# A state-space block ahead of an MLP: where one chunk's decay banks, its score and mix products and a set of transposes stand in the queues

## The chip, the core and the metric

The kernel runs on one core of a Trainium2 chip. A core has five engines with a queue each: PE (matrix products; its weight loads are listed apart as PEld), DVE (VectorE), ACT (ScalarE), POOL (GpSimd) and SP, which here only starts transfers. Each engine works through its own queue in the order in which the program issued it, and waits at an instruction until what it needs is there. PE writes into PSUM, eight banks of 128 x 512 float32 values; DVE and ACT read them there.

The metric is the device time of one execution in microseconds (us). Before the change it is 372.75 us, the median of 6 runs (371.79 to 374.67).

## What is computed

Inputs are x (4 batches, 8 heads, 768 tokens, 32 values), a decay `a` for each batch, head and token, and B and C with 16 state values for each. The reference works in chunks of tokens:

```python
log_a = np.log(np.clip(a, 1e-06, 1.0))
cum = np.cumsum(la, axis=-1)                      # la: log_a of the chunk
L = np.exp(cum[:, :, :, None] - cum[:, :, None, :]) * causal
CB = np.einsum('bhin,bhjn->bhij', Cc, Bc)
y_intra = np.einsum('bhij,bhjd->bhid', CB * L, xc)
y_inter = np.einsum('bhin,bhnd->bhid', Cc, state) * decay_to_i[:, :, :, None]
y[:, :, sl] = y_intra + y_inter                   # and the state is carried on
```

The result, 3072 tokens of 256 values, goes through an MLP: h = y @ w_in (256 to 2048), g = h * clip(h + 3, 0, 6) / 6, out = g @ w_out (2048 to 256). The weights come as float64 and are turned into float32 on the chip.

## The kernel before

It takes 6 chunks of 128 tokens for all 4 batches at once, and works the MLP of chunk k beside the attention of chunk k+1. The order on every engine is the order of the program (`tc.manual_schedule()`, L68); tiles of one tag share a fixed number of buffers, and a new tile waits until the one whose room it takes is no longer read.

**PSUM.** Tag "f" has four banks, "o" two, "y0" and "y1" one each. [...]

**Decays of chunks 0 and 1.** L is kept as [token j, head, token i], a pair of batches to a tile. For chunk 0 and for batches 0 and 1 of chunk 1 it is made by PE: a bank `d` holds half of a batch's heads (b is the batch, u the half). `diff_mask` (L272) chooses the bank and writes the causal mask; `diff_add` (L286) adds the differences of the running sums in five small matmuls; `diff_exp` (L297) is ACT's exponential into L. Chunk 0's banks are f, f, f, f, o, o, y0, y1; chunk 1's are all "o". `diff_fill(b, u)` (L711) is mask and add for chunk 1, `diff` (L678) all three at once.

**Attention of chunk 0.** `turn(0, p)` (L335) transposes B and C of two batches into one "f" bank (eight transposes for both p) and copies them out: `bT` by ACT, `cT` by DVE for p = 0 and by ACT for p = 1. `scores(0, (b,))` (L369) makes the products of C and B for one batch in four "f" banks `cb` (32-row matmuls), and DVE multiplies them into L (L384). `mix(0, (b,))` (L387) multiplies L with x into the two "y" banks, 32 columns at a time. `keep(0, p)` (L423) has ACT copy two batches to `yT` and DVE take the new state. `ends` (L317) is POOL's product for that state.

**Weights.** `weights(i, n)` (L673) takes n steps of `decode(i)` (L154): (1) ACT copies the top words, (2) three DVE operations, (3) an ACT pass, (4) an ACT pass and a DVE product (L178), after which `load_w(i + 3)` is issued on SP, (5) two DVE operations, of which the last writes a quarter of w_in (i below 4) or w_out. Three raw buffers are used in turn.

**MLP of chunk 0.** `mlp_in(0, f)` (L445) makes one of 16 blocks of h with four matmuls of w_in on PE; ACT and DVE make gT of it (L524, L529). The list `weave` puts decode steps between the blocks. `first_out` (L533) multiplies gT with w_out into `o`. The tile gT of chunk 0 takes the room of `pre` (tag "gT", one buffer), in which the running sums `cum` of all chunks lie.

**by_token** (L260) has PE transpose the running sums of chunks 1 to 5 out of `pre` (five small transposes into one "o" bank, `c_ps`), and DVE write them negated to `cum_n`, which the exponentials of later chunks read from batch 2 of chunk 1 on (L312). In the kernel before it stands in the MLP of chunk 0 behind block f = 1.

The sequence around the change (L698 to L740) is written out by hand:

Of the kernel before, what the change touches and what calls it, by code (L numbers as in the profile page):

```python
# [20 lines left out]
def kernel(  # L21
# [238 lines left out]
    def by_token():  # L260
        c_ps = ps_o.tile([P, NC, G], FP32, name="c_ps", tag="o")
        for c in range(1, NC):
            nc.tensor.transpose(out=c_ps[:, c], in_=cum_c[:, c], identity=ident[:G, :G])
        nc.vector.tensor_scalar(
            out=cum_n[:, 1:], in0=c_ps[:, 1:], scalar1=-1.0, scalar2=None, op0=ALU.mult)
# [6 lines left out]
    def diff_mask(c, b, u):  # L272

        k = 2 * b + u
        if c == 0 and k < 4:
            d = ps.tile([P, HU, P], FP32, name="d", tag="f")
        elif c == 0 and k >= 6:
            d = ps_y.tile([P, HU, P], FP32, name="d", tag=f"y{u}")
        else:
            d = ps_o.tile([P, HU, P], FP32, name="d", tag="o")  # L280
        nc.tensor.matmul(
            out=d, lhsT=ident_h, rhs=hide.unsqueeze(1).to_broadcast([P, HU, P]),
            start=True, stop=True)
        ds[c, b, u] = d
# [12 lines left out]
    def diff_exp(c, b, u):  # L297
        nc.scalar.activation(
            decays_of(c, b)[:, HU * u:HU * u + HU], ds.pop((c, b, u)), AF.Exp)
# [14 lines left out]
    def from_start(c):  # L314
        nc.scalar.activation(etos[c], etos[c], AF.Exp)
# [19 lines left out]
    def turn(c, p):  # L335


        bc, xt = loaded[c]
        pool, tag = (ps, "f") if c < 2 else (ps_o, "o")
        t_ps = pool.tile([P, 4, P], FP32, name="t_ps", tag=tag)  # L340
        for k in range(4):
            j, b = k // 2, 2 * p + k % 2
            nc.tensor.transpose(  # L343
                out=t_ps[:, k],
                in_=bc[:, j, b * NH:(b + 1) * NH].rearrange("s h n -> s (h n)"), identity=ident)
        bT = att.tile([P, 2, P], FP32, name="bT")
        nc.scalar.copy(out=bT, in_=t_ps[:, 2:4])
        if c == 1 and p == 0:
            from_start(c)
            carry(c)  # L350
            for b in range(NB):
                ends(c, b)
        cT = att.tile([P, 2, 2, P], FP32, name="cT")
        if c == 1 or (c, p) == (0, 1):
            for t in range(2):
                nc.scalar.activation(
                    cT[:, :, t], t_ps[:, 0:2], AF.Copy, scale=parity[:, t:t + 1])
        else:
            nc.vector.tensor_tensor(
                out=cT, in0=t_ps[:, 0:2].unsqueeze(2).to_broadcast([P, 2, 2, P]),  # L360
                in1=parity.unsqueeze(1).unsqueeze(3).to_broadcast([P, 2, 2, P]), op=ALU.mult)
        csT = None
        if c:
            csT = att.tile([P, 2, P], FP32, name="csT")
            nc.vector.tensor_tensor(
                out=csT, in0=t_ps[:, 0:2], in1=etos[c][:, 2 * p:2 * p + 2], op=ALU.mult)
        bTs[c, p] = bT, cT, csT
# [305 lines left out]
    def weights(i, n):  # L673
        for _ in range(n):
            next(parts[i], None)


    def diff(c, b, u):  # L678
        diff_mask(c, b, u)
        diff_add(c, b, u)  # L680
        diff_exp(c, b, u)
# [20 lines left out]
    ends(0, 0)  # L702
    diff_exp(0, 1, 0)
    weights(0, 2)
    for b, u in ((2, 0), (2, 1), (1, 1), (3, 0)):
        diff_exp(0, b, u)
    for b in range(NB - 1):
        ends(0, b)
# [2 lines left out]
    def diff_fill(b, u):  # L711
        diff_mask(1, b, u)
        diff_add(1, b, u)

    diff_fill(0, 0)
    diff_fill(0, 1)
    turn(0, 0)
    turn(0, 1)
    diff_exp(0, 3, 1)
    ends(0, 3)  # L720
    diff_exp(1, 0, 0)
    diff_exp(1, 0, 1)
    weights(1, 1)
    scores(0, (0,))
    scores(0, (1,))
# [2 lines left out]
    mix(0, (1,))  # L728
    keep(0, 0)
    scores(0, (3,))  # L730
    diff(1, 1, 0)
    mix(0, (2,))
    mix(0, (3,))
    weights(1, 1)
    diff_fill(1, 1)
    keep(0, 1)
    diff_exp(1, 1, 1)
    weights(1, 3)
    load_eto(1)
    load(1)  # L740
# [7 lines left out]
    for k in range(NC):  # L748
        gTs[k] = ffn.tile([P, NF, TB], FP32, name="gT")
        c, ahead = k + 1, k + 2  # L750
        if k == 0:
            for f in range(NF):
                mlp_in(k, f)
                for i in weave.get(f, []):
                    weights(i, 1)
                if f == 1:
                    by_token()
                if f in (6, 8):
                    b = f // 2 - 1
                    load_decay(c, b)  # L760
                    conceal(c, b)
            load(ahead)
            weights(NP + 1, 1)
            weights(NP + 3, 1)
            weights(NP + 2, 3)
            sums, sums_in = weight_sums(), in_weight_sums()
            for i in range(NP):
                for b in range(NB):
                    first_out(b, i)
                    if (i, b) == (0, 0):  # L770
                        weights(NP + 3, 1)
                        weights(NP + 2, 1)
                        weights(NP + 3, 3)
                        rows(ahead)
                        decay(c, 2)
                        decay(c, 3)
                    elif (i, b) == (1, 0):
                        next(sums_in)
                    elif (i, b) == (2, 0):
                        turn(c, 0)  # L780
                        turn(c, 1)
                        for b_ in range(NB):
                            conceal(ahead, b_)
                    elif (i, b) == (2, 1):
                        scores(c, (0, 1))
                        next(sums_in)
                    elif (i, b) == (2, 2):
                        decay_ends(ahead, 0)
                        next(sums)
                        next(sums)  # L790
                    elif (i, b) == (2, 3):
                        results(c, 0)
                        scores(c, (2, 3))
                        decay_ends(ahead, 1)
                    elif (i, b) == (3, 0):
                        next(sums)
                        decay_ends(ahead, 2)
                    elif (i, b) == (3, 1):
                        results(c, 1)
                        sum_y(c)  # L800
                        decay_ends(ahead, 3)
                        from_start(ahead)
                    elif (i, b) == (3, 2):
                        lead(c, 0)
            rows(ahead + 1)
            continue
        for s in range(NJ):
            early(k, s)
            if s == 0:
                if ahead < NC:  # L810
                    load(ahead)
                if c < NC:
                    carry(c)
            if s < NJ - 1:
                lead(k, s + 1)
            if s:
                last(k, s - 1)
                ramp(k, 2 * s - 2, evens[k, s - 1])
            middle(k, s)
            if s:  # L820
                times_ramp(k, 2 * s - 2, evens[k, s - 1])
            ramp(k, 2 * s + 1, odds[k, s])
            times_ramp(k, 2 * s + 1, odds[k, s])
            if s in (1, 3) and ahead < NC:
                conceal(ahead, s - 1)
                conceal(ahead, s)
            if s in (3, 5) and c < NC:
                turn(c, s // 4)
            if s in (2, 4, 6):
                g_sums(k, s - 2)  # L830
        for i, _ in enumerate(out_units(k)):
            if i == 0:
                s = NJ - 1
                last(k, s)
                ramp(k, 2 * s, evens[k, s])
                times_ramp(k, 2 * s, evens[k, s])
                g_sums(k, s - 1)
                if k == 1:
                    next(sums)
            if c < NC:  # L840
                if i in (2, 4):
                    if i == 4:
                        results(c, 0)
                    scores(c, ((0, 1), (2, 3))[i // 4])
                if ahead < NC and i in (2, 3, 5, 6):
                    decay_ends(ahead, {2: 0, 3: 1, 5: 2, 6: 3}[i])
                    if i == 6:
                        from_start(ahead)
                if i == 7:
                    results(c, 1)  # L850
                    sum_y(c)
                    if ahead + 1 < NC:
                        rows(ahead + 1)
                if i == 12:
                    lead(c, 0)
# [30 lines left out]
```

## Time and profile before

| what | us |
|---|---|
| median of 6 runs | 372.75 |
| the six runs | 374.67, 371.98, 372.48, 373.22, 373.02, 371.79 |
| the profiled execution's time | 374.67 |
| its span, first to last instruction | 373.0 |
| PE busy in it | 364.1 (98%) |
| PE weight loads busy | 308.2 (83%) |
| DVE busy | 229.1 (61%) |
| ACT busy | 190.5 (51%) |
| POOL busy | 134.3 (36%) |

The profile is of the first of the six runs. A row of it gives an instruction or a group of like ones by engine and source line, the tile written and those read, and in brackets for how long the engine had been idle before it and what ended that. "granted clock" is the share of the TensorE clock that the chip's throttle let through. Times are counted from the span's start. A busy PE need not be one at its peak, since its matmuls overlap and their ends are modelled.

By stages of the span: until about 10 us the running sums and chunk 0's differences are made; until about 27 us chunk 0's attention; until about 55 us h of chunk 0; until about 90 us its output, with the attention of chunk 1 between; then five like stages of about 57 us each.

### The profile page before, as it was taken

The numbers are of one execution on the slowest core, as the hardware profiler recorded it, in microseconds if no ns is written. First come the engines' busy times: TensorE is split into PE (matmuls) and PEld (weight loads), VectorE is DVE, ScalarE is ACT, GpSimd is POOL, SyncE is SP. The second block draws the span as 40 slices with busy tenths as digits, with TensorE's granted clock in tenths as the row PEclk, the third lists the DMA queues.
The fourth block names the chain that finished last, engine by engine and source line by source line (L and its number), as shares of the span: only waits on it lengthen the run. The fifth ranks groups of instructions, "written<-read, shape, count | busy, mean of one in ns | idle before, by whom it ended". The sixth has DMA issues, their size and how long they took to land.

```text
span 373.0 us, 7275 instructions
## 1 busy us (share of the span) xinstructions
PE 364.1 (98%) x2893; PEld 308.2 (83%) x2893; DVE 229.1 (61%) x448; ACT 190.5 (51%) x414; POOL 134.3 (36%) x134
## 2 busy tenths in 40 slices
PE   7799999999999999999999999999999999999996
PEld 3464448878788999888999888999888989988996
DVE  7577999987588452588343588342488433388211
ACT  5748868958575560466560466660376100376100
POOL 1200020262289712079703069700057900047800
PEclk9889999999999999999999999999999999999999
DMA  9957999900894007840008860000000000000000
GB/s 165 212 207 164 150 335 152 268 6 28 272 85 43 2 30 251 98 47 0 2 13 270 89 57 0 2 2 30 28 3 1 2 2 30 28 1 2 2 28 28
DMA packets 86690, 29.21 MB, mean 78 GB/s; under 512 B 75457, under 2 KB 81249, under 8 KB 86657
## 3 DMA queue, kind: packets, MB, share of 16 engines
q1 hardware_dynamic: 86656, 28.76, 38.3%
q8 instruction: 22, 0.36, 0.4%
q14 instruction: 12, 0.09, 0.1%
HBM read 25.53 MB, written 3.23 MB: 77 GB/s over the span
## 4 chain that ended last, share of the span: by engine, by line
PE 84%; DVE 7%; ACT 6%; DMA 1%; issue 1%; SPq 0%; ACTq 0%
PE even L490 19%; PE ob L599 17%; PE oa L599 17%; PE odd L490 14%; PE cb L376 4%; PE y L409 4%; PE o L540 3%; DVE gT L529 2%; DVE wm L178 2%; PE y L400 2%; ACT we L175 2%; DMA raw<-in_moe_w_in_dram 1%; ACT L L312 1%; PE t_ps L343 1%; PE h L448 1%; ACT gT L524 1%
## 5 line engine op out<-in xcount | busy, mean ns | idle before, releaser
L585 POOL TENSOR_TENSOR s<-gT 128x512 f32<-128x512 f32 x20 | 26.4, 1321 | 105.5 <-DVE gT L529 105.5
L490 PE MATMUL even<-ts,w_sum 128*128 128x256 f32 x160 | 48.2, 383 | 0.0
L524 ACT ACTIVATE gT<-odd,half 128x512 f32<-128x512 f32 x40 | 27.5, 687 | 35.4 <-DVE odd L517 35.4
L503 ACT COPY even<-odd 128x512 f32<-128x512 f32 x40 | 23.0, 575 | 43.0 <-PE odd L490 42.1
L312 ACT ACTIVATE L<-L,cum_n 128x128 f32<-128x128 f32 x144 | 43.2, 392 | 2.1 <-POOL L L303 2.1
L384 DVE TENSOR_TENSOR L<-L,cb 128x512 f32<-128x512 f32 (+1 forms) x56 | 30.4, 605 | 18.4 <-PE cb L376 18.4
L490 PE MATMUL odd<-yT,w_in 128*128 128x256 f32 x160 | 41.1, 379 | 0.0
L599 PE MATMUL oa<-w_out,gT 128*128 128x128 f32 x320 | 39.3, 278 | 0.0
L599 PEld LDWEIGHTS oa<-w_out,gT 128*128 128x128 f32 x320 | 38.1, 192 | 1.4 <-issue 0.2
L599 PE MATMUL ob<-w_out,s 128*128 128x128 f32 x320 | 37.8, 276 | 0.0
L599 PEld LDWEIGHTS ob<-w_out,s 128*128 128x128 f32 x320 | 36.5, 192 | 1.3 <-issue 1.3
L303 POOL TENSOR_SCALAR_AFFINE_SELECT L<-L 128x1024 f32<-128x1024 f32 x18 | 19.9, 1122 | 48.6 <-DMA L<-cum_d 48.4
L490 PEld LDWEIGHTS even<-ts,w_sum 128*128 128x128 f32 x160 | 29.9, 190 | 5.3 <-ACT up L510 1.5
L529 DVE SCALAR_TENSOR_TENSOR gT<-gT,odd 128x512 f32<-128x512 f32 x40 | 27.5, 688 | 9.9 <-ACT gT L524 9.8
L490 PEld LDWEIGHTS odd<-yT,w_in 128*128 128x128 f32 x160 | 30.1, 190 | 3.9
L524 ACT ACTIVATE gT<-even,half 128x512 f32<-128x512 f32 x40 | 27.8, 694 | 4.4 <-PE even L490 4.4
L529 DVE SCALAR_TENSOR_TENSOR gT<-gT,even 128x512 f32<-128x512 f32 x40 | 27.1, 678 | 4.4 <-ACT gT L524 4.4
L599 PE MATMUL ob<-t,gT 128*128 128x128 f32 x240 | 29.7, 277 | 0.0
L599 PEld LDWEIGHTS ob<-t,gT 128*128 128x128 f32 x240 | 28.0, 192 | 1.3 <-issue 1.3
L540 PE MATMUL o<-w_out,gT 128*128 128x256 f32 x128 | 29.0, 382 | 0.1
L504 DVE COPY up<-odd 128x256 f32<-128x256 f32 x40 | 16.9, 422 | 18.2 <-ACT even L503 14.4
L448 PE MATMUL h<-yT,w_in 128*128 128x512 f32 x64 | 27.9, 594 | 0.0
(110 smaller groups left out, 635.0 us busy)
## 6 DMA issues: line engine op xcount, KB each, us to landing
L<-cum_d SPq DMA_DIRECT2D x18, 512.0 KB, 6.1
raw<-in_moe_w_in_dram SPq DMA_DIRECT2D x4, 1024.0 KB, 8.3
raw<-in_moe_w_out_dram SPq DMA_DIRECT2D x4, 1024.0 KB, 7.2
xt<-in_x_dram SPq DMA_DIRECT2D x6, 512.0 KB, 8.6
out_dram<-res SPq DMA_DIRECT2D x20, 128.0 KB, 1.7
bc<-in_C_dram SPq DMA_DIRECT2D x6, 256.0 KB, 5.1
bc<-in_B_dram SPq DMA_DIRECT2D x6, 256.0 KB, 7.5
eto<-cum_d SPq DMA_DIRECT2D x40, 32.0 KB, 4.8
```

Of the source, the lines that this page charges most:

```text
L303: nc.gpsimd.affine_select(out=L, in_=L, pattern=[[0, NH], [1, P]], compare_op=ALU.is_ge, fill=-1e5, base=0, channel_multiplier=-1)
L312: nc.scalar.activation(L[:, h], L[:, h], AF.Exp, bias=cum_n[:, c, g:g + 1])
L384: nc.vector.tensor_tensor(out=L[:, :, hs], in0=L[:, :, hs], in1=cbs[q][:, in_pair], op=ALU.mult)
L448: nc.tensor.matmul(out=h.rearrange("p r i -> p (r i)"), lhsT=w_in[:, j, f * P:(f + 1) * P], rhs=yTs[k][:, j].rearrange("p b i -> p (b i)") ...
L490: nc.tensor.matmul(out=bank[:, r], lhsT=lhsT, rhs=rhs, start=start, stop=True, skip_group_check=True)
L503: nc.scalar.copy(out=even, in_=odd[:, 1:2].to_broadcast([P, 2, 2 * P]))
L504: nc.vector.tensor_copy(out=up[:, 1], in_=odd[:, 0])
L524: nc.scalar.activation(gTs[k][:, f], h.rearrange("p r i -> p (r i)"), AF.Relu, bias=half, scale=1.0 / 6.0)
L529: nc.vector.scalar_tensor_tensor(out=g, in0=g, scalar=1.0, in1=h.rearrange("p r i -> p (r i)"), op0=ALU.min, op1=ALU.mult)
L540: nc.tensor.matmul(out=o[:, b % 2], lhsT=gTs[0][:, f, b * P:(b + 1) * P], rhs=w_out[:, f], start=(f == 0 and b % 2 == 0), stop=True, skip_ ...
L585: nc.gpsimd.tensor_tensor(out=o, in0=p_, in1=q_, op=op)
L599: nc.tensor.matmul(out=bank[:, slot], lhsT=lhs[:, j], rhs=rhs[:, j], start=(clear and j == 0), stop=True, skip_group_check=True)
```

## The change

It touches one choice of bank and the order of calls; no operation is added or removed, and none changes its size.

- Chunk 1's banks for batch 0 (k below 2) take tag "f" instead of "o"; those for batch 1 stay with "o".
- Chunk 0's exponential (3, 0) moves from ahead of the transposes to behind them.
- The exponentials of chunk 1's batch 0 move from behind the transposes to ahead of them on ACT.
- Bank (1, 0) of chunk 1 is filled ahead of the transposes, bank (1, 1) behind them; before, they were filled between the mixes and behind the last mix. Their exponentials move ahead of the scores.
- `by_token` moves from behind block f = 1 of h to behind the last mix, ahead of two of quarter 1's decode steps.

```diff
     def diff_mask(c, b, u):
         k = 2 * b + u
-        if c == 0 and k < 4:
+        if k < (4 if c == 0 else 2):
             d = ps.tile([P, HU, P], FP32, name="d", tag="f")
         elif c == 0 and k >= 6:
             d = ps_y.tile([P, HU, P], FP32, name="d", tag=f"y{u}")
...
-    for b, u in ((2, 0), (2, 1), (1, 1), (3, 0)):
+    for b, u in ((2, 0), (2, 1), (1, 1)):
         diff_exp(0, b, u)
...
     diff_fill(0, 0)
     diff_fill(0, 1)
+    diff_exp(1, 0, 0)
+    diff_exp(1, 0, 1)
+    diff_fill(1, 0)
     turn(0, 0)
     turn(0, 1)
-    diff_exp(0, 3, 1)
+    diff_fill(1, 1)
+    for c, b, u in ((0, 3, 0), (0, 3, 1), (1, 1, 0), (1, 1, 1)):
+        diff_exp(c, b, u)
     ends(0, 3)
-    diff_exp(1, 0, 0)
-    diff_exp(1, 0, 1)
     weights(1, 1)
     scores(0, (0,))
     scores(0, (1,))
     mix(0, (0,))
     scores(0, (2,))
     mix(0, (1,))
     keep(0, 0)
     scores(0, (3,))
-    diff(1, 1, 0)
     mix(0, (2,))
     mix(0, (3,))
+    by_token()
     weights(1, 1)
-    diff_fill(1, 1)
     keep(0, 1)
-    diff_exp(1, 1, 1)
     weights(1, 3)
...
                 for i in weave.get(f, []):
                     weights(i, 1)
-                if f == 1:
-                    by_token()
```

## The prediction

> **What bounds the kernel now.** I read the windows first, because the change touches only the first 35 us; then the rows of PE, ScalarE and VectorE there; then what follows, to see whether a shift survives. Window columns: stretch and length, busy time (instructions) of PE, PE's weight loads, DVE, ACT and POOL, granted TensorE clock, DMA share, GB/s.
>
> ```profile
> 8.90:12.30 3.40, 1.41 (x15) 0.82 (x13) 2.54 (x4) 3.40 (x6) 0.00 (x0) 1.00 1.28 104
> 12.30:15.70 3.40, 3.40 (x19) 2.64 (x18) 1.14 (x1) 1.47 (x4) 1.84 (x4) 0.50 1.45 157
> 15.70:19.10 3.40, 2.90 (x19) 1.82 (x17) 2.49 (x7) 2.59 (x7) 0.41 (x1) 1.00 0.98 387
> 19.10:22.50 3.40, 3.40 (x47) 1.99 (x48) 1.38 (x5) 1.13 (x1) 0.00 (x0) 0.51 1.04 425
> 30.40:55.20 24.80, 24.76 (x62) 10.96 (x62) 23.51 (x35) 19.82 (x25) 1.42 (x2) 1.00 1.07 227
> ```
>
> Two stretches run at half clock. From 30.40 PE has no gap, with DVE beside it at 23.51 of 24.80. So the end is set by when the dense stage h (64 matmuls, L448) begins, by what interrupts it, and by whether DVE keeps up. The rows, PE first, then ACT, then DVE (start, length, operation, idle time before it and its releaser):
>
> ```profile
> 12.00 0.38 PE L281 MATMUL d<-hide,ident_h 128*128 128x512 bf16 x1 [1.99 <-ACT L L298]
> 16.49 3.17 PE L376 MATMUL cb<-cT,bT 32*128 32x256 f32 x16 [0.48 <-DVE cT L359]
> 24.24 0.39 PE L281 MATMUL d<-hide,ident_h 128*128 128x512 bf16 x1
> 25.57 0.62 PE L409 MATMUL y<-L,xt 128*32 128x128 f32 x16
> 26.24 0.39 PE L281 MATMUL d<-hide,ident_h 128*128 128x512 bf16 x1
> 26.90 3.60 PE L448 MATMUL h<-yT,w_in 128*128 128x512 f32 x8
> 30.43 0.49 PE L263 MATMUL c_ps<-ident,pre 32*128 32x32 f32 x5
> 55.21 15.78 PE L540 MATMUL o<-w_out,gT 128*128 128x256 f32 x72
> ```
>
> ```profile
> 11.35 2.06 ACT L298 ACTIVATE L<-d 128x512 f32<-128x512 f32 x4
> 15.34 0.37 ACT L347 COPY bT<-t_ps 128x256 f32<-128x256 f32 x1 [1.93 <-PE t_ps L343]
> 19.18 1.13 ACT L165 COPY ws<-raw 128x1024 uint16<-128x1024 uint16 x1 [0.56 <-DMA raw<-in_moe_w_in_dram]
> 30.96 0.69 ACT L524 ACTIVATE gT<-h,half 128x512 f32<-128x512 f32 x1 [1.04 <-PE c_ps L263]
> ```
>
> ```profile
> 15.75 0.69 DVE L359 TENSOR_TENSOR cT<-t_ps,parity 128x512 f32<-128x512 f32 x1 [2.31 <-ACT bT L347]
> 23.72 1.41 DVE L384 TENSOR_TENSOR L<-L,cb 128x256 f32<-128x256 f32 x4
> 25.05 0.42 DVE L167 TENSOR_SCALAR we<-ws 128x1024 uint16<-128x1024 uint16 x1
> 35.29 0.32 DVE L264 TENSOR_SCALAR cum_n<-c_ps 128x160 f32<-128x160 f32 x1
> ```
>
> PE stands idle for 1.99 us until an exponential frees a "o" bank; ACT then idles for the transposes; gT of the first feature block idles 1.04 us for by_token, since gT lies in the room of `pre`, which by_token reads.
>
> **1. The first banks.** Chunk 1's banks (0,0) and (0,1) take "f" banks freed early, so they follow the last matmul at 9.85 (9.63 plus its 0.22 pace). A bank costs 0.66 at full clock (24.24 to 24.91): done by 11.2. Bank (1,0) takes the "o" bank and waits until 12.00 as now; the idle time shrinks to 0.8. At full clock it ends at 12.66 and the eight transposes (1.04 in the row at 70.82) by 13.75; B's load (issued at 2.21, 10.6 to landing) is there at 12.85. ACT now has five exponentials from 11.35 at a pace of 0.48, to 13.79: it, not PE, is late next. Then bT 0.37, cT 0.69 and two hand-overs of 0.04: scores begin at 14.92, 1.57 earlier. Bank (1,1) (0.66) is over by 14.4, in PE's wait for cT.
>
> Is the clock full there? [...] The rows say otherwise: 1.41 busy of 3.40 was followed by 0.50. The stretch before it, which was to be followed by full clock, was 2.57 busy of 3.40 (5.50:8.90). With the two banks the same stretch becomes about 2.6 busy. I follow the rows: full clock after 12.3. [...]
>
> **2. Exponentials.** Four (pace 0.48) now follow cT's ACT copies, from 15.1 to 17.1. The next ACT work is the weight copy that waits for its load until 19.18: free, with 2 us of cover. Two that stood at 25.11 and 27.10 leave ACT (0.48 each).
>
> **3. Scores and mixes with nothing between.** Of the two removed banks, 24.24's delayed mix(3): its L was ready at 25.14, it began at 25.57, so 0.4, not 0.66. The one at 26.24 ran to 26.90 while yT's first half was ready at 26.74: 0.1. Walking the queue from 14.92 by the same rows: L products start 0.81 later (16.49 to 17.30) at a pace of 0.333, eight done at 18.5; mix(0) at 17.8 takes 0.57 at full clock (25.00 to 25.57), not 1.22; scores(2) at 18.4, its L at 19.1 to 20.5; mix(1) (1.2) and scores(3) (1.23) I charge at half clock, since a low stretch of 32-row matmuls was followed by 0.51 before; last L 21.65 to 23.07; mix(3) at 23.1; yT's copy 0.8 later, as now, ready at 24.27; **h at 24.35 instead of 26.90: 2.55.**
>
> **4. by_token ahead of h.** Its PE time leaves h: 0.43 (30.43 to 30.86); ahead of h it lies in the wait for yT (free; 0.4 if that were gone). gT's 1.04 wait goes. Against it: on DVE, cum_n (0.32) waits for mix(3) and the five transposes, and behind it stand the weight operations that ran at 25.05 to 26.54 in the shadow of mixes. They now start at 24.54, DVE idling 1.1. Then ACT's two passes (to 27.25) and gT at 27.25, 3.7 earlier; quarter 1 of w_in at 29.35 against h's need at 24.35 + 4×1.72 = 31.2: cover 1.9. DVE's next quarter starts 3.4 earlier, and 0.32 less lies in the saturated part, so DVE stays ahead of PE: the 0.27 that PE lost to w_out (54.94 to 55.21) goes too.
>
> On SP nothing is added, but the load of weight quarter 4 waits for DVE's product of quarter 1: 27.4 instead of 28.2, only 0.8 earlier. Behind it go eto, chunk 1's loads, and quarter 5 (issued at 40.06, 9.0 to landing: 49.1, used at 51.60). That use moves to 48.3, the landing to 48.3: a cover of 2.5 is spent. Bounds: nothing, to 1 us on ACT; I take nothing, as the walk gives just in time.
>
> **Sum** for the profiled execution: 2.55 + 0.43 + 0.27 = 3.25. From o on, PE runs 72 matmuls without a gap behind the same weight chain, so the shift stays: span 373.0 to 369.75, its time 374.67 to **371.4**.
>
> **Against the median.** The profiled run is the slowest of six, 1.92 above the median. With neither half-clock stretch, my walk of the old order gives scores at 15.15, and h at 23.84 because the weight copy at 19.18 holds yT back: 3.06 less, 371.6, near the lowest run, 371.79. The new order without them: h at 23.55, so 0.3 + 0.43 + 0.27 = 1.0 less: 370.6. So old runs spread between 371.6 and 374.7, new ones mostly between 370.6 and 371.4, some above. **Forecast 371.2**, 1.55 under the median, 0.4%.
>
> **Rivals.** (a) The half-clock stretch stays at 12.3, or moves onto the scores: 1.05 less gain, 372.5 in the profiled run's terms, some 372.1 at the median. For it: nothing but 32-row and 32-column matmuls from 14.4 to 23.7. Against: 2.6 busy of 3.4. Chance 0.17. (b) All 3.25 come off the median: 369.5. For: each step has a row; against: the lowest run already lacks most of it. 0.13. (c) Slower: half clock falls on h. The banks at 24.24 and 26.24 were full-width work just before h; without them the stretch before h is thinner. A stretch of 3.41 at half clock in gap-free work costs 1.7: 371.4 + 1.7 = 373.1; it is slower than before once 2.7 of the stretch lies in h. Against: h itself is dense and at 22.5 the clock came back after a stretch with the same matmuls. 0.12. (d) Quarter 5 lands late and ACT stalls one for one, 372.5 for 1.1 late; 0.08. The forecast has 0.5.
>
> **Numbers.** About 0.5% (1.86 us) is what a measurement tells from no change. Faster than 370.9: (b) and four tenths of the forecast's own spread, and a little of the unknown below it, 0.35. Slower than 374.6 needs (c) and (d) together, or a wait that I do not see: 0.10. The rest, 0.55. The range 369.9 to 373.1 takes in (a), (c) and (d) and leaves out (b).
>
> **What would show it.** Right: a wait of about 0.8 at PE's third bank; bT near 13.8; scores near 14.9; no d bank between cb and y; h near 24.3; no c_ps inside h; gT near 27.3 with no wait for c_ps; o near 52. Wrong: clock 0.5 in h or at 12.3; a DMA named before ws at 48; DVE, not PE, still late at o. If h begins under 1 us earlier, step 1 or 3 is wrong.

## The result, and the profile after

The changed kernel takes 370.23 us at the median (369.79 to 373.9), the kernel before, measured beside it, 372.99. The ratio is 0.9929, 95% interval 0.9913 to 0.9944: 0.71% faster. The forecast was 371.2, 0.4% faster, with a range from 369.9 to 373.1.

The profiled execution of the changed kernel took 371.23 us with a span of 369.5. The walk had said 371.4 for an execution like this one. The windows, in the columns of before (stretch and length, busy time of PE, weight loads, DVE, ACT and POOL, granted clock, DMA share, GB/s):

```profile
8.90:12.30 3.40, 3.21 (x33) 2.10 (x32) 2.55 (x4) 3.40 (x6) 0.00 (x0) 1.00 1.28 98
12.30:15.70 3.40, 2.87 (x27) 1.94 (x23) 1.79 (x3) 3.40 (x10) 1.85 (x4) 1.00 1.47 172
14.10:17.50 3.40, 2.58 (x17) 1.75 (x16) 2.54 (x7) 2.90 (x7) 1.01 (x3) 1.00 1.15 307
17.50:20.90 3.40, 3.40 (x50) 2.15 (x52) 1.38 (x5) 1.11 (x1) 0.00 (x0) 0.51 1.05 417
24.50:52.00 27.50, 27.50 (x64) 12.13 (x65) 26.83 (x40) 22.31 (x28) 1.44 (x1) 1.00 0.91 184
```

PE is busy for 3.21 us of the stretch 8.90:12.30, in which it had 1.41, the clock is full after it, and one half-clock stretch is left of the two, on the scores and mixes. The dense stage is PE without a gap, DVE beside it at 26.83 of 27.50. The timeline of PE, then ACT, then DVE (start, length, operation, idle time before it and what ended that):

```profile
11.87 0.38 PE L281 MATMUL d<-hide,ident_h 128*128 128x512 bf16 x1 [0.19 <-ACT L L298]
14.81 0.99 PE L376 MATMUL cb<-cT,bT 32*128 32x256 f32 x8 [0.53 <-DVE cT L359]
23.96 0.49 PE L263 MATMUL c_ps<-ident,pre 32*128 32x32 f32 x5
24.50 27.73 PE L448 MATMUL h<-yT,w_in 128*128 128x512 f32 x64
52.07 15.70 PE L540 MATMUL o<-w_out,gT 128*128 128x256 f32 x72
```

```profile
11.23 2.54 ACT L298 ACTIVATE L<-d 128x512 f32<-128x512 f32 x5
13.62 0.69 ACT L347 COPY bT<-t_ps 128x256 f32<-128x256 f32 x2
18.67 1.11 ACT L165 COPY ws<-raw 128x1024 uint16<-128x1024 uint16 x1 [1.67 <-DMA raw<-in_moe_w_in_dram]
27.41 0.67 ACT L524 ACTIVATE gT<-h,half 128x512 f32<-128x512 f32 x1
```

```profile
24.48 0.32 DVE L264 TENSOR_SCALAR cum_n<-c_ps 128x160 f32<-128x160 f32 x1 [1.04 <-PE c_ps L263]
24.73 0.42 DVE L167 TENSOR_SCALAR we<-ws 128x1024 uint16<-128x1024 uint16 x1
```

Scores begin at 14.81 instead of 16.49, h at 24.50 instead of 26.90, o at 52.07 instead of 55.21. c_ps stands ahead of h, so h is one row of 64. ACT's first gT has no wait any more. The price is in DVE's rows: it idles 1.04 us for c_ps, and the weight operations come behind it.

The executions say more than the medians. Each gives a mean granted clock, and one stretch of 3.41 us at half clock (17.54 to 20.95 in the changed kernel's profile) takes 0.0046 off the mean of a span of 370 us. So they fall into groups by the number of such stretches (0.998 and above, about 0.995, 0.990, 0.986; of the profiled executions e7's has none at 0.999, the changed kernel's one at 0.995, that of before two at 0.991, and e10's 10.2 us of half clock at 0.986). Executions and their median time in each (five of the kernel before, at 0.982 and over 377 us, belong to a slower state and are left out):

| half-clock stretches | 0 | 1 | 2 | 3 | mean number |
|---|---|---|---|---|---|
| before | 18: 371.75 | 27: 372.99 | 19: 374.19 | 21: 375.84 | 1.5 |
| changed | 37: 370.16 | 7: 371.52 | 3: 372.25 | 1: 373.90 | 0.33 |

Two effects add up. At equal clock the change is worth 1.5 to 1.9 us (371.75 to 370.16 with no stretch, 372.99 to 371.52 with one, 374.19 to 372.25 with two). And a stretch, which costs 1.2 to 1.7 in the kernel before, has become rare: 1.17 fewer on average, some 1.5 us by an estimate from this table.

The table mixes chips: the counts before come from three, and the chip of 36 of the 48 changed executions is not on record. On one chip, beside e8, the counts were 9, 10, 4, 4 and 9, 1, 2, 0, and the gain without a stretch was 1.3 (371.61 to 370.34). The share of executions without a stretch differs between chips: for the kernel before it was 4 of 33 on the chip of e1 to e4, 5 of 25 on that of e5 to e7, and 9 of 27 on that of e8 to e10.

### The profile page after: what moved, and what is told of

It reads as the page before. It is cut to its first block, busy times and chain, and to the rows that moved or that the text cites. A ratio compares the mean times of both kernels' runs of the same rounds, so it can differ in the third digit from the quotient of the medians.

```text
span 369.5 us, 7275 instructions
## 1 busy us (share of the span) xinstructions
PE 362.2 (98%) x2893; PEld 307.5 (83%) x2893; DVE 229.0 (62%) x448; ACT 190.1 (51%) x414; POOL 134.7 (36%) x134
## 4 chain that ended last, share of the span: by engine, by line
PE 82%; DVE 8%; ACT 6%; DMA 1%; issue 1%; SPq 0%; ACTq 0%
PE even L490 19%; PE ob L599 17%; PE oa L599 17%; PE odd L490 14%; PE cb L376 4%; PE y L409 4%; PE o L540 3%; DVE gT L529 2%; DVE wm L178 2%; ACT we L175 2%; PE y L400 2%; DMA raw<-in_moe_w_in_dram 1%; ACT L L312 1%; ACT L L298 1%; PE t_ps L343 1%; DVE w_out L191 1%
```

## The experiments

Theories: **clock** (PE's idle time ahead of the scores brings on half clock, and filling it is most of the gain at the median), **queue** (the gain is the waits taken out of the order; half clock comes and goes by chance), and for each part of the change, whether its own rows give its worth.

**e1: by_token back.**

```diff
-    by_token()
     weights(1, 1)
...
+                if f == 1:
+                    by_token()
```

> The changed kernel with by_token back behind block f = 1 of h, all else as changed. If by_token's place is worth what its rows say (0.43 us of PE inside h, and the wait of gT for it, of which 0.27 reached PE), this is 0.4 to 0.7 us slower than the changed kernel, so some 2.1 to 2.4 us under the kernel before. If gT's wait of 1.04 us is the main gain of the change, it is over 1 us slower than the changed kernel. If by_token does not matter, it is within 0.2 us of it.

Measured: 372.29, ratio to before 0.996 (0.9934 to 0.9987). Without a half-clock stretch 371.69 (6 executions) against 370.16; with one 372.61 (4) against 371.52: 1.1 to 1.5 us, about twice what the rows of before gave. The banks alone change the clock: 6 of 12 executions have no stretch, against 4 of 33 of the kernel before on that chip. Its timeline, ACT and then PE:

```profile
25.90 1.15 ACT L177 ACTIVATE we<-we,bias_lo 128x1024 uint16<-128x1024 bf16 x1
28.76 0.69 ACT L524 ACTIVATE gT<-h,half 128x512 f32<-128x512 f32 x1 [1.71 <-PE c_ps L263]
```

```profile
24.60 3.70 PE L448 MATMUL h<-yT,w_in 128*128 128x512 f32 x8 [0.47 <-ACT yT L432]
53.12 15.81 PE L540 MATMUL o<-w_out,gT 128*128 128x256 f32 x72 [0.17 <-DVE w_out L191]
68.77 1.04 PE L343 MATMUL t_ps<-ident,bc 128*128 128x128 f32 x8
72.91 1.12 PE L376 MATMUL cb<-cT,bT 32*128 32x256 f32 x10 [0.29 <-DVE csT L365]
```

The same two places in the changed kernel's timeline of PE:

```profile
67.61 1.04 PE L343 MATMUL t_ps<-ident,bc 128*128 128x128 f32 x8
71.39 1.12 PE L376 MATMUL cb<-cT,bT 32*128 32x256 f32 x10 [0.31 <-DVE csT L365]
```

From h to o it is 28.52 (24.60 to 53.12) against 27.57: 0.95, more than c_ps's 0.43 and the 0.27. ACT is ready at 27.05 and now waits 1.71 for c_ps, DVE begins its next weight quarter at 31.68 instead of 30.61, and PE waits for w_out at 53.12. The lateness of ACT and DVE shows once more at chunk 1's transposes: from them to the second row of scores it is 4.14 against 3.78, another 0.36.

**e2: by_token alone**, in the kernel before.

```diff
     mix(0, (3,))
+    by_token()
     weights(1, 1)
     diff_fill(1, 1)
...
-                if f == 1:
-                    by_token()
```

> The kernel before with only by_token moved behind the last mix. It stands there ahead of the bank at 26.24, which holds h back already, so its 0.43 us of PE stay on the path; what is left is the 0.27 us and gT's earlier start. Expected 0.2 to 0.5 us under the kernel before by my sum; no gain or a loss would mean that the move pays only once that bank is gone. A gain over 1 us would make by_token the cause of most of the change's effect.

Measured: 373.68, ratio 0.9991 (0.9951 to 1.0031), not to be told from before. Without a stretch 371.23 (3) against 371.75: 0.5 us, on few executions. PE's timeline shows why it is little:

```profile
24.60 0.49 PE L263 MATMUL c_ps<-ident,pre 32*128 32x32 f32 x5
25.02 0.39 PE L281 MATMUL d<-hide,ident_h 128*128 128x512 bf16 x1
...
25.69 4.88 PE L448 MATMUL h<-yT,w_in 128*128 128x512 f32 x11
```

c_ps and the bank d stand one behind the other ahead of h, whose yT was ready earlier (its copies began at 24.73 and last 0.65). So most of the 0.43 is only moved while that bank is there: by an estimate from these rows h could have begun near 25.4, and it begins at 25.69. Behind that the move works as meant, with 27.55 from h to o (25.69 to 53.24) against 28.31 before. These 0.76 less the 0.3 lost ahead of h are about the 0.5 measured. The mean number of half-clock stretches is 1.8, no fewer than before.

**e3: the first two banks and by_token**, the other two banks back where they were.

```diff
     diff_exp(1, 0, 1)
-    diff_fill(1, 0)
     turn(0, 0)
     turn(0, 1)
-    diff_fill(1, 1)
...
     scores(0, (3,))
+    diff(1, 1, 0)
     mix(0, (2,))
...
     weights(1, 1)
+    diff_fill(1, 1)
     keep(0, 1)
+    diff_exp(1, 1, 1)
```

> The changed kernel with chunk 1's two banks of batch 1 back between the mixes and behind the last one; the first two banks still follow chunk 0's. Clock theory (PE's idle gap at 10 to 12 us brings on half clock, and filling it is most of the gain at the median): at least 1.5 us under the kernel before, and most runs with a granted clock of 0.998 or more. Queue theory (the waits removed between scores and mixes are most of the gain): no more than 1 us under it, and granted clocks as before.

Measured: 372.84, ratio 0.9986 (0.9961 to 1.0011), and none of 12 executions without a half-clock stretch (mean 1.9). As written, the clock theory failed here: with the two banks behind chunk 0's alone, and by_token, no gain at the median is told from noise and half clock is no rarer. Its timeline and windows tell why:

```profile
12.71 1.17 PE L343 MATMUL t_ps<-ident,bc 128*128 128x128 f32 x8
15.06 0.98 PE L376 MATMUL cb<-cT,bT 32*128 32x256 f32 x8 [1.18 <-DVE cT L359]
```

```profile
9.70:16.50 6.80, 5.32 (x50) 3.63 (x49) 4.38 (x6) 6.58 (x14) 2.00 (x5) 1.00 1.33 152
16.50:23.30 6.80, 6.80 (x72) 4.72 (x72) 3.96 (x12) 1.76 (x3) 0.27 (x1) 0.50 1.02 408
```

The idle time ahead of the transposes is closed, helped by first sums at half pace until 9.7 in this profile (four take 0.63 us at 8.76 and 0.39 at 10.09). But idle time now stands behind them (1.18), and the scores fall to half clock (0.50) for 6.8 us. In the changed kernel it is bank (1, 1) that stands there (idle 0.53). At equal clock e3 is slower than the changed kernel by 1.1 with one stretch (372.62 against 371.52), 0.5 with two (372.76 against 372.25) and 1.1 with three: the place of the other two banks is worth 0.5 to 1.1, on few executions.

**e4: the kernel before, with PE kept busy** from 9.85 to 12.00.

```diff
             diff_add(0, b, u)
+    for _ in range(3):
+        ds_again(0, 3, 1)     # mask and adds of one bank once more
     load_w(1)
```

> The kernel before, with chunk 0's last bank of differences made four times over instead of once: three more masks and adds (2.0 us of PE) stand in PE's idle gap from 9.85 to 12.00, and nothing else is changed or moved. Clock theory: though it does more work, it is 0.8 to 1.6 us faster at the median than the kernel before, its slowest runs (over 375 us) go, and the fastest runs stay at about 371.2 to 371.6. Queue theory: same time as before or up to 0.2 us slower, with the same spread.

Measured: 373.55, ratio 0.998 (0.9944 to 1.0016). By time neither theory is told: the clock theory's gain of 0.8 to 1.6 did not come, and three executions still take over 375. By clock the filling works: 9 of 12 executions have no half-clock stretch, where before has 4 of 33 on the same chip. This is the clearest run for the clock theory, since nothing but the filling differs. But these nine spread from 371.69 to 374.28 with a median of 372.68, so up to 2.6 us are lost otherwise. In the profiled execution, which has full clock throughout, the repeats fit the gap:

```profile
12.30:15.70 3.40, 2.65 (x27) 1.96 (x25) 1.77 (x2) 2.80 (x8) 1.85 (x4) 1.00 1.46 162
15.70:19.10 3.40, 3.26 (x45) 2.15 (x41) 2.74 (x8) 1.62 (x4) 0.41 (x1) 1.00 1.01 401
```

Where the first sums run at half pace for longer (in e5's profile four still take 0.63 us at 10.50, and 0.39 at 11.21), the first banks end late, and the 2 us of repeats stand in the way instead of in a gap. That this is the loss in the other executions is argued, not shown, as no profile of one was taken.

**e5: less work in the same order.** Each of chunk 1's four banks gets its mask only.

```diff
     def diff_fill(b, u):
         diff_mask(1, b, u)
-        diff_add(1, b, u)
```

> The changed kernel, with chunk 1's four banks given only their mask: the five matmuls of differences of each are left out (0.44 us of PE a bank, 1.76 in all), so L of chunk 1's batches 0 and 1 lacks the decay. The order is that of the changed kernel. Clock theory: PE is idle for some 3 us instead of 1.2 before the scores, so half-clock stretches come back (a granted clock of 0.995 or less in most runs), and with less work it is 1 to 2.5 us slower than the changed kernel at the median, 0 to 1.5 us under the kernel before; a run without such a stretch is near 370.2. Queue theory: with less work and the same order it is as fast as the changed kernel or up to 0.3 us faster, some 2.7 us under the kernel before.

Measured: 371.55, ratio 0.9946 (0.9914 to 0.9978). With less work it is slower at the median than the changed kernel, by 0.9 to 1.3 (370.67 in e8, 370.23); three of 12 executions have no stretch and take 370.21, as the changed kernel does, and the mean number is 1.25 against 0.33. So without a stretch the sums cost nothing that shows. That they keep the clock full follows less surely, as e5 ran on another chip than e8. On its own chip e7, with more work in the same places, has no stretch in 9 of 12 executions, but e6, with the changed kernel's banks whole, in only 3 of 9. So e5 against e7 speaks for the clock theory, and e5 against e6 (mean number 0.89) does not tell. Its windows:

```profile
14.50:17.90 3.40, 2.79 (x24) 1.95 (x28) 2.54 (x8) 2.49 (x6) 0.62 (x2) 1.00 1.08 334
17.90:21.30 3.40, 3.40 (x59) 2.34 (x51) 1.62 (x6) 1.10 (x1) 0.00 (x0) 0.50 1.03 412
```

**e6: the decode steps ahead of by_token**, so that DVE does not wait for c_ps first.

```diff
     mix(0, (3,))
-    by_token()
     weights(1, 1)
+    by_token()
     keep(0, 1)
```

> The changed kernel with the two neighbouring calls swapped: the three weight operations on VectorE ahead of by_token, so that they no longer stand behind cum_n and its wait of 1.04 us. If that wait costs something at the end, this is 0.1 to 0.4 us faster than the changed kernel (quarter 1 of w_in and its successor load come 0.5 to 1 us earlier). If PE is the only bound there, as I hold, it is within 0.15 us of it.

Measured: 370.98, ratio 0.9921 (0.9889 to 0.9954). Without a stretch 370.05 (3), with one 371.17 (4): 0.1 to 0.35 under the changed kernel, on few executions. In the profile h runs from 24.47 and o from 52.04, the same 27.57 as in the changed kernel. PE is the bound there, and DVE's wait costs little or nothing. Only 3 of 9 executions have no stretch, though the swap stands behind the scores and mixes where this profile's half pace lies (the 16 matmuls of a mix take 1.08 us at 19.78, 0.65 at 22.04); whether the chip makes this, no run tells.

**e7: the changed kernel with the last gaps filled**, by one repeat of e4's kind in each.

```diff
+    ds_again(0, 3, 1)
     diff_fill(1, 0)
     turn(0, 0)
     turn(0, 1)
     diff_fill(1, 1)
+    ds_again(0, 3, 1)
```

> The changed kernel with chunk 0's last bank of differences made three times over: one repeat (0.66 us of PE) in each of the two idle gaps that are left before the scores (about 0.55 us each). Clock theory: fewer runs with a half-clock stretch than the changed kernel's 8 of 36, none or one of 12, and the others 0 to 0.3 us later for the work that the gaps do not hold. Queue theory: 0.1 to 0.3 us slower, with as many runs of a lower granted clock.

Measured: 371.36, ratio 0.9937 (0.9907 to 0.9968); 9 of 12 executions without a stretch, at 371.19, which is 0.8 to 1.0 above the changed kernel's (370.34 in e8, 370.16). The clock theory's none or one of 12 with a stretch did not come: there are three, about the changed kernel's share elsewhere (11 of 48), but fewer than e6's six of nine on this chip. The profiled one is early, with h at 23.29 and o at 50.86, 1.2 ahead of the changed kernel's profile, yet its span of 369.1 is only 0.4 shorter. The timeline of PE, then of DVE (line numbers are 6 higher, as a helper was added):

```profile
91.37 1.03 PE L496 MATMUL odd<-yT,w_in 128*128 128x256 f32 x4
93.33 0.70 PE L496 MATMUL even<-yT,w_sum 128*128 128x256 f32 x2 [0.94 <-DVE odd L523]
```

```profile
91.98 0.42 DVE L510 COPY up<-odd 128x256 f32<-128x256 f32 x1 [3.98 <-DMA out_dram<-ob]
```

DVE waits for a store to land, as `up` and the output tile `ob` share two buffers, and then PE waits for DVE.

This profile and e4's both have full clock throughout, one in the new order and one in the old, and both have the bank ahead of the transposes begin at the same time (11.93 and 11.94). So they give the worth of the order itself. PE's rows of h and o, in e4 and then in e7:

```profile
24.18 3.60 PE L454 MATMUL h<-yT,w_in 128*128 128x512 f32 x8
52.27 15.70 PE L546 MATMUL o<-w_out,gT 128*128 128x256 f32 x72
```

```profile
23.29 27.73 PE L454 MATMUL h<-yT,w_in 128*128 128x512 f32 x64
50.86 15.70 PE L546 MATMUL o<-w_out,gT 128*128 128x256 f32 x72
```

h begins 0.89 earlier and o 1.41 earlier. In e4 the bank between scores and mixes holds mix(2) from 21.52 to 22.27; in e7 mix(2) follows the scores at 21.40.

**e8: the changed kernel again**, beside e9 and e10.

> The changed kernel itself once more, beside the kernel before and the next two on one chip: some 2.8 us under the kernel before at the median, most runs with a granted clock of 0.998 or more and near 370.2.

Measured: 370.67, ratio 0.9932 (0.99 to 0.9963); 9 of 12 without a stretch, at 370.34.

**e9: three buffers behind that tag.**

```diff
-    ... name="up", tag="ob", bufs=2)
+    ... name="up", tag="ob", bufs=3)
-    ob = ffn.tile([P, 2, DM], FP32, name="ob", bufs=2)
+    ob = ffn.tile([P, 2, DM], FP32, name="ob", bufs=3)
```

> The changed kernel with three buffers instead of two behind tag ob, which the output tile ob and MLP's tile up share (L500, L544); nothing else. In the changed kernel's profile DVE waits 3.0 us for the landing of ob before it can write up, at 92.3, and PE has just no gap there; where the stages before are earlier, as in e7, PE loses 0.94 us there. If this landing holds back the runs that begin h early, the runs with full clock come 0.4 to 0.9 us under the changed kernel's, some 369.4 to 369.8, and those with one half-clock stretch hardly change. If it does not, no run changes by more than 0.2 us.

Measured: 370.55, ratio 0.9937 (0.9903 to 0.9972); without a stretch 370.22 (8) against e8's 370.34. The wait for the store is gone from DVE's timeline, and the time has not moved:

```profile
91.61 0.42 DVE L504 COPY up<-odd 128x256 f32<-128x256 f32 x1 [2.39 <-ACT even L503]
```

So in the changed kernel that landing is not what keeps executions at full clock from being faster.

**e10: e7 and e9 together.**

> e7 (two repeats of one bank in the idle gaps) with the three buffers of e9. With a full clock and without the wait for ob, e7's profile loses its gap of 0.94 us: some 0.8 us under e7, so near 370.5 at the median, and its runs near 369.4 at the best; with as few half-clock stretches as e7. If the repeats cost what the gaps do not hold, it stays 0.3 us or more above e9.

Measured: 370.36, ratio 0.9937 (0.9903 to 0.997); 10 of 12 executions without a stretch, at 370.35. It is 0.8 under e7 without a stretch, some 0.2 of which may be the chip (the kernel before has 371.84 there and 371.61 here). So most of what e7 lost was the wait for the store, not its repeats. It is no better than e8 or e9. None of these versions beats the change by more than the measurement tells.

What was not tried: the change without its first part (the two banks of batch 0 left in "o"). e3 shows no gain from this part without the banks around the transposes; whether those need it is open.

## Why the prediction was right, and where it fell short

**The walk of the queues held.** Predicted and found in the profiled execution: bT at 13.79 and 13.62, scores at 14.92 and 14.81, h at 24.35 and 24.50, gT at 27.25 and 27.41 with no wait for c_ps, o at 51.95 and 52.07, the time 371.4 and 371.23. PE's wait at the third bank, put at 0.8, was 0.35. Part of that is luck: in this execution the first sums ran at half pace until 7.3, so the last of chunk 0 came at 9.99 instead of 9.63. It also lifts PE's busy time in the stretch, which step 1 put at about 2.6 (its own rows give 2.7), to 3.21. ACT, not PE, was late next, as said. The four exponentials before the weight copy were covered (ACT idle 1.67 there). The weight load on SP, for which a cover of 2.5 us was to be spent and no more, was in time: ACT's copy at 48.31 has no wait. That answers rival (d).

**The step that failed is "Against the median".** It charged one half-clock stretch to most executions of the changed kernel and put them "mostly between 370.6 and 371.4". Of 48 executions 37 have none and stand at 370.16. The forecast took the profile's remaining stretch for a fixture of the order because low 32-row work had been followed by one in the profile before. It was one case of several. The kernel before was read rightly: 371.6 was said for an execution without a stretch, and 371.75 is measured.

**Two terms were mis-sized at equal clock.** The order without any stretch was to gain 1.0; it gained 1.6 by the table, 1.3 on one chip, and 1.41 at o between the profiles of e4 and e7. The step is in the sum 0.3 + 0.43 + 0.27: the 0.3 for the start of h is 0.89 in those profiles. Step 3 charged the bank between scores and mixes at 0.4, for a mix(3) that waits on DVE; at full clock L is ready and the bank holds mix(2) for its whole 0.75.

The other term is by_token's place, put at 0.43 + 0.27 = 0.70. Taken back alone (e1) it is 1.1 to 1.5, since gT's wait lasts longer once h starts earlier (1.71 instead of 1.04), makes the stretch from h to o 0.95 longer and leaves ACT and DVE late at chunk 1's transposes (0.36).

The parts do not add. by_token alone gives 0.5 (e2), the banks without by_token nothing when there is no stretch (e1's 371.69 against 371.75) and 0.4 with one, both together 1.3 to 1.6. Each leaves the other's delay on the path: with the bank ahead of h, c_ps is mostly moved; with c_ps inside h, an earlier h only makes gT wait longer.

**The clock's reason was right, its place half right.** Step 1 followed the rows of before, where half clock (0.50) comes after PE has idled for 1.99 us. The runs bear it out: in the profiles of e3 and e5 half clock follows gaps of 1.18 and 0.81 (0.50 in both), and e4's work in the gap keeps it away in 9 of 12 executions. But step 1 gave the credit to the two banks behind chunk 0's. e3 has those and falls to half clock in every execution; e1, which has all four, does so in half of them, on the same chip. So the banks around the transposes are needed; whether they would do alone is open.

**The rivals.** (a) meant a stretch beyond the one that step 3 had already charged to the scores and mixes. In full it can be the case only in the 4 of 48 executions with two or more. Of the seven with one, two have a profile: the changed kernel's shows just the charged stretch (17.54 to 20.95), and e8's is past its one by 23.04, with a mix of 16 in 0.65 us there and h in 27.73. The 1.05 that the forecast gave this rival was the author's estimate, and no run shows that term; between the changed kernel's groups one stretch is worth 1.36 (370.16 to 371.52). (b), all 3.25 off the median, overstates it: 2.76 came off. (c), half clock on h, did not decide the change's time; it was seen once, in e10 (below). So a gain called 0.4% was 0.7%: the charged stretch mostly did not come, and the order itself was worth 0.3 to 0.6 more than its 1.0. The measured 370.23 lies below 370.9, to which the prediction gave a chance of 0.35.

## What to carry to other kernels

Before explaining one profile, sort the executions by their mean granted clock: how often a stretch at half clock comes and what a kernel takes without one are two effects of one edit, and a single trace shows one draw. Here work that had to be done anyway was best put where PE idled ahead of thin work (37 of 48 executions without a half-clock stretch, 18 of 85 before), and the gap behind it has to be looked at too: with only the first filled, e3 still idled for 1.18 us behind the transposes and fell to 0.50. Two small delays that stand one behind the other on the same path are to be removed together; either alone shows little.

## What the runs showed of the hardware that had not been expected

The half-clock stretches of these profiles differ in length: 3.41 us each in the kernel before (12.31 to 15.72 and 19.14 to 22.55) and in the changed one (17.54 to 20.95), 6.8 in e3 and 10.2 in e10, by their windows. What sets a stretch's start or length no run shows.

The first sums run at half pace up to a time that differs by execution: until 7.3 in the changed kernel (four take 0.58 us at 6.17 and 0.39 at 7.58), 9.7 in e3, 11.1 in e5, where four sums of chunk 0 still took 0.63 us at 10.50 (before has 0.39 for them from 6.34 on). The granted-clock column reads 1.00 there all the same, so the mean clock does not count this start. The operations and their order alone do not fix the number of stretches: the kernel before has none to three in the table, and e2, whose work is that of before up to the last mix, has one in its profile (mean clock 0.995) where before has two (0.991).

In these profiles PE's busy time in the stretch ahead alone doesn't tell whether half clock follows. In e4 2.65 of 3.40 us (12.30:15.70) were followed by full clock, in e5 2.79 of 3.40 (14.50:17.90) by half. The former was partly full-width banks and transposes, the latter nearly all 32-row scores and 32-column mixes. But scores and mixes alone were followed by full clock too: 3.26 of 3.40 in e4 (15.70:19.10), with 1.00 from 19.10 to 22.50.

Half clock also lasted longer and fell on dense work: e10's profiled execution (375.40 us) has, by its windows,

```profile
20.60:30.80 10.20, 10.20 (x98) 6.30 (x91) 6.85 (x17) 3.68 (x7) 0.00 (x0) 0.50 0.28 107
```

10.2 us of it, with h from 26.89 on inside, and PE busy all the time. The 64 matmuls of h took 29.66 us there, 27.73 in the changed kernel. Rival (c)'s half clock on h thus came once, though no filling of gaps explains it there.
